# Attention heads one step deeper in the pipeline, and a bias by distance that goes through memory

## The chip, the cores and the metric

One core of a Trainium2 chip runs the whole program in one launch. The metric is device time in microseconds: 544.67 is the median of 3 runs of the kernel before (543.47 to 544.70). The engines are TensorE (PE; its weight loads are the row PEld), VectorE (DVE), ScalarE (ACT), GpSimd (POOL), and SyncE (SP), which issues the transfers.

## What is computed

Three stages, all in float32, with B=2, H=8, S=576, D=64, 32 hidden units:

```
scores = q @ k^T / sqrt(D)
x      = log1p(|i - j|) / log1p(max(i, 1))
bias   = relu(x * w1 + b1) @ w2            # for each head, row i and column j; the same for both batches
attn   = softmax(scores + bias);  o = attn @ v
y      = (o @ w_a * (o @ w_b)) @ w_out     # 1152 tokens, 512 -> 1536 -> 512
out    = LN(h * softmax(h)) * g @ w_out2,  h = y @ w_in    # 512 -> 1024 -> 512
```

Only the first stage is touched by the change. Its bias depends on the row i and the distance |i - j|.

## The kernel before

**Units and steps.** The 576 rows are four tiles of 128 and a tail of 64. A unit is one tile with one batch (the tail takes both batches), nine in all; a step is one head of one unit, 72 in all. A loop over n (line 635) walks the steps and in each emits parts in the order of a string (`ORDER`, line 27): a letter stands for one part, applied to the head of n or of some steps earlier. Each engine executes its instructions in the order in which they were emitted.

**One head.** `scores` (letter s, head n) makes the scores in PSUM (L400). `biased` (b, head n-1) adds the bias tile on VectorE and takes the minimum (the signs are turned), tile `e` (L419). `powers` (p, n-1) is the exponential with its row sum on ScalarE (L426). `summed_powers` (a, n-1) puts the sum into `rec` on GpSimd (L430). `shares` (h, n-2) takes the reciprocal on VectorE (L435) and multiplies the row by it on GpSimd (L436). `turned` (t, n-3) transposes on TensorE (L444, L453) and copies to SBUF. `values` (v, once in two steps) multiplies by V for two heads (L473). `scores` and the bias sums share a pool of two PSUM slots (`ps_s`).

**The bias.** It is made for 16 rows at a time; such a set is called T, 36 in all (8 to a tile, 4 in the tail). `bias_hidden` makes four hidden tiles of 128 x 576 from windows of a table `tabs` (L356 on VectorE, L358 on ScalarE, by the letters v and a of `HIDDEN`: 3 and 1 for T 0 to 7, all four on VectorE for T 8, 18 of 28 on VectorE for T 9 to 15, 28 of 32 for T 16 to 31, 14 of 16 for the rest). `bias_sums` sums them over the hidden units: 4 x 2 matmuls of 288 columns into one PSUM slot, four of them side by side in groups of 32 columns of the array (L366). `bias_out` scales them into SBUF (`st`, L376) and SP sends them to the bias tile, SBUF to SBUF, 288 KB (L385; twice for the tail). Two bias tiles exist (`big`). Tile 0 is made before the steps begin; T 9 to 15 have their sums at steps 5, 7, 9, 10, 12, 13, 14 (`SECOND_T`), T 16 on every second step from 16 to 46, the last four at 48, 50, 52, 54 (`LAST_T`). The hidden parts come one and two steps ahead of the sums, `bias_out` one step behind.

**Around it.** K, V and q are fetched by SP in the same queue. K is doubled on VectorE and transposed on TensorE until step 11. In the last unit the first expert weights are unpacked (`first_one`), and three products of the second stage (`gated`, L132) are emitted at steps 72, 74 and 75, among the last heads (`EARLY`).

Of the kernel before, what the change touches and what calls it, by code (L numbers as in the profile page):

```python
# [54 lines left out]
def tile_kernel(ctx, tc, q, k, v, w1, b1, w2, w_a, w_b, w_out, w_in2, w_out2, g_ln, psi, rpsi, out):  # L55
# [108 lines left out]
    with ExitStack() as actx:  # L164
# [35 lines left out]

        def table(a, n, row, at, pool, tag):

            w = (n + 1) // 2
            halves = []
            for i in range(2):
                m = min(w, n - i * w)
                ps = pool.tile([P, 512], F32, tag=tag, name=f"table_{a}_{i}")
                for g in range(4):
                    o = a + i * w - 4 * g - at
                    nc.tensor.matmul(ps[g * HID:(g + 1) * HID, 0:m], w1r, row[:, o:o + m], start=True, stop=True)  # L210
                halves.append((tb[:, a + i * w:a + i * w + m], ps[:, 0:m]))
            return halves

        halves_r = table(half, UW - half, psi_r, half - 12, ps_s, "s")
# [127 lines left out]
        def place(T):  # L342

            it, r = divmod(T, P // 16)
            return it, 64 * (r // 4), r % 4

        def bias_hidden(T, quads=range(4)):

            it, r, c = place(T)
            for qd in quads:  # L350
                t0 = it * P + r + 16 * qd
                h = hp.tile([P, S], F32, tag="h", name=f"h_{T}_{qd}")
                win = tb[:, OFF - t0 - c:OFF - t0 - c + S]
                sc = nb[:, c, t0 // 16:t0 // 16 + 1]
                if HIDDEN[min(it, 2)][T % len(HIDDEN[min(it, 2)])][qd] == "v":
                    nc.vector.tensor_scalar(h, win, sc, 0.0, op0=ALU.add, op1=ALU.max)  # L356
                else:
                    nc.scalar.activation(h, win, AF.Relu, bias=sc)  # L358
                bias_w.setdefault(T, []).append(h)

        def bias_sums(T):

            bps = ps_s.tile([P, 2, 512], F32, tag="s", name=f"bps_{T}")
# [5 lines left out]
        def bias_out(T, send=True):  # L369

            it, r, c = place(T)
            if it not in bias_t:
                bias_t[it] = big.tile([P, H, S], F32, tag="big", name=f"bias_{it}")
            st = stp.tile([P, S], F32, tag="st", name=f"st_{T}")
            k = 9 * c + 2 * it + r // 64
            nc.scalar.activation(st.rearrange("p (a j) -> p a j", a=2), bias_w.pop(T)[:, :, 0:SH], AF.Copy, scale=rp[:, k:k + 1])  # L376
            bias_w[T] = st
            if send:
                bias_sent(T)

        def bias_sent(T):
            it, r, c = place(T)
# [102 lines left out]

        units = [(it, [b]) for it in range(NC) for b in range(B)] + [(NC, list(range(B)))]

        qs = {}
        extra, sums_at, out_at, keep_at, low_at = {}, {}, {}, {}, {}

# [21 lines left out]
        for w in first_in:  # L512
            fetch(w)
        nc.sync.dma_start(psi_l, psi[3:4, low + 3 - 12:half + 3])
        N0 = P // 16
        for T in range(N0 + 2):
            if T == N0:
                nc.scalar.copy(*halves_l[0])
                nc.vector.tensor_copy(*halves_l[1])
            if T <= N0:  # L520
# [5 lines left out]
            if T == N0 - 2:  # L526
                halves_l = table(low, half - low, psi_l, low - 12, ps_t, "t")
            if T > 0:
# [471 lines left out]
```

## Time and profile before

| | us |
|---|---|
| median of 3 runs | 544.67 |
| the profiled execution | 544.01 |
| its span, first to last instruction | 542.2 |
| TensorE busy | 530.4 |
| VectorE busy | 419.1 |
| ScalarE busy | 286.1 |
| GpSimd busy | 156.5 |

The granted clock of TensorE is 1.0 of full speed all along. A matmul's end is modelled, so a TensorE that is busy all the time is not necessarily at its peak; the times from start to start say more. In the span the first bias and K are made until 27.8 us, the heads run until 212.4 us, and the other stages fill the rest.

### The profile page before, as it was taken

The page shows a single profiled execution, that of the slowest core. Times are in us where ns is not written, and L with a number is a line of the kernel's source. Part 1 is how long each engine was busy: PE and PEld are TensorE (multiplying, and loading weights), DVE is VectorE, ACT ScalarE, POOL GpSimd, SP SyncE. Part 2 cuts the span into 40 slices and gives each one's busy share as a digit, 9 for nine tenths or more (in the row PEclk, how much of TensorE's full clock was granted, in tenths as well). Part 3 has the DMA queues.
Part 4 walks back from the last instruction along what each step waited for, and adds up shares of the span by engine and source line. Part 5 has one row for each costly group of instructions (what it writes and reads, how often), then busy time and mean ns, then how long its engine had stood idle before and what let it go on. Part 6 is the DMA issues. An engine that isn't in the chain of part 4 may idle for free.

```text
span 542.2 us, 12391 instructions
## 1 busy us (share of the span) xinstructions
PE 530.4 (98%) x4873; PEld 471.8 (87%) x4873; DVE 419.1 (77%) x904; ACT 286.1 (53%) x598; POOL 156.5 (29%) x262
## 2 busy tenths in 40 slices
PE   7989999999999999999999999999999999999997
PEld 3667788888878899999999999999999988888886
DVE  5988889999886794887899798897884467656661
ACT  5878887788886663555565334522534332232321
POOL 3034445554456630222222122242224330000000
PEclk9999999999999999999999999999999999999999
DMA  4995533333266012444553443444300000000011
GB/s 93 208 197 127 115 82 86 78 73 79 69 151 181 3 41 82 154 144 128 156 153 121 117 155 117 128 144 152 118 4 2 0 1 20 21 19 21 19 31 48
DMA packets 53918, 49.32 MB, mean 91 GB/s; under 512 B 31583, under 2 KB 44132, under 8 KB 53861
## 3 DMA queue, kind: packets, MB, share of 16 engines
q1 hardware_dynamic: 53584, 48.52, 33.1%
q8 instruction: 38, 0.62, 0.5%
q14 instruction: 20, 0.16, 0.1%
q10 hardware_dynamic: 276, 0.02, 0.0%
HBM read 34.37 MB, written 2.36 MB: 68 GB/s over the span
## 4 chain that ended last, share of the span: by engine, by line
PE 83%; DVE 8%; issue 3%; ACT 3%; POOL 1%; DMA 1%; SPq 0%; ACTq 0%; DVEq 0%; POOLq 0%
PE pm L132 26%; PE po L132 11%; PE py L897 9%; PE ph L837 9%; PE bps L366 6%; PE px L473 6%; PE s L400 5%; PE pt L444 5%; DVE e L419 2%; PE pl L878 1%; ACT e L426 1%; PE tp_q L290 1%; DVE et L449 1%; PE tp_k L290 1%; DMA arena_hi<-in_k_dram 1%
## 5 line engine op out<-in xcount | busy, mean ns | idle before, releaser
L102 POOL TENSOR_SCALAR f<-f 128x512 f32<-128x512 f32 x48 | 41.5, 866 | 138.3 <-ACT f L98 127.3
L132 PE MATMUL pm<-xhi,abh 128*128 128x384 f32 x240 | 80.2, 334 | 0.0
L132 PE MATMUL pm<-xhi,abl 128*128 128x384 f32 x240 | 80.2, 334 | 0.0
L132 PE MATMUL pm<-xlo,abh 128*128 128x384 f32 x240 | 80.2, 334 | 0.0
L426 ACT ACTIVATE e<-e,nm 128x576 f32<-128x576 f32 x72 | 56.0, 777 | 32.2 <-DVE nm L419 30.8
L436 POOL TENSOR_SCALAR e<-e,rec 128x576 f32<-128x576 f32 x72 | 53.8, 747 | 28.7 <-DVE rec L435 26.2
L419 DVE CUSTOM_DVE_ANT_0 e<-s,bias 128x576 f32<-128x576 f32 x72 | 53.9, 750 | 2.6 <-DMA arena_hi<-in_k_dram 1.3
L356 DVE TENSOR_SCALAR h<-tabs 128x576 f32<-128x576 f32 x116 | 55.0, 515 | 0.3
L132 PE MATMUL po<-gh,oh 128*128 128x384 f32 x144 | 48.5, 337 | 0.8 <-DVE x2s L768 0.8
L151 ACT COPY one<-pm 128x384 f32<-128x384 f32 x36 | 17.2, 478 | 60.9 <-PE pm L132 60.7
L132 PE MATMUL po<-gh,ol 128*128 128x384 f32 x144 | 48.4, 336 | 0.0
L132 PE MATMUL po<-gl,oh 128*128 128x384 f32 x144 | 48.4, 336 | 0.0
L366 PE MATMUL bps<-h,w2bd 128*32 128x288 f32 x576 | 45.7, 420 | 1.2 <-DVE h L356 1.0
L444 PE MATMUL pt<-ident,e 128*128 128x128 f32 x288 | 45.1, 279 | 0.4 <-POOL e L436 0.4
L132 PEld LDWEIGHTS pm<-xhi,abl 128*128 128x128 f32 x240 | 45.1, 188 | 0.0
L132 PEld LDWEIGHTS pm<-xhi,abh 128*128 128x128 f32 x240 | 45.0, 188 | 0.0
L132 PEld LDWEIGHTS pm<-xlo,abh 128*128 128x128 f32 x240 | 45.0, 188 | 0.0
L114 DVE SCALAR_TENSOR_TENSOR f<-words,f 128x512 int32<-128x512 int32 x48 | 42.8, 891 | 1.6
L430 POOL TENSOR_SCALAR rec<-sums 128x1 f32<-128x1 f32 x72 | 20.9, 290 | 79.2 <-ACT e L426 78.9
L400 PE MATMUL s<-kst,qhi 128*128 128x288 f32 x160 | 40.6, 335 | 2.4 <-DVE nm L419 2.4
L473 PE MATMUL px<-et,vsb 128*32 128x128 f32 (+1 forms) x1280 | 40.5, 264 | 0.2 <-DVE et L449 0.2
L473 PEld LDWEIGHTS px<-et,vsb 128*32 128x32 f32 x1280 | 33.8, 110 | 7.5 <-issue 2.1
(137 smaller groups left out, 1247.8 us busy)
## 6 DMA issues: line engine op xcount, KB each, us to landing
bias<-st SPq DMA_DIRECT2D x40, 288.0 KB, 3.6
words<-in_moe_w_out_dram SPq DMA_DIRECT2D x20, 512.0 KB, 3.6
words<-in_moe_w_a_dram SPq DMA_DIRECT2D x12, 512.0 KB, 3.6
words<-in_moe_w_b_dram SPq DMA_DIRECT2D x12, 512.0 KB, 3.4
words<-in_moe_w_in_dram SPq DMA_DIRECT2D x8, 512.0 KB, 3.7
nat_q<-in_q_dram SPq DMA_DIRECT2D x16, 128.0 KB, 3.2
arena_hi<-in_k_dram SPq DMA_DIRECT2D x16, 128.0 KB, 2.5
vsb<-in_v_dram SPq DMA_DIRECT2D x16, 128.0 KB, 2.6
```

The source lines that it names most:

```text
L114: nc.vector.scalar_tensor_tensor(out=b, in0=words[:, :, 0], scalar=29, in1=b, op0=ALU.logical_shift_right, op1=ALU.bitwise_or)
L132: nc.tensor.matmul(ps, w, x, start=(i == 0), stop=(i == n - 1))
L356: nc.vector.tensor_scalar(h, win, sc, 0.0, op0=ALU.add, op1=ALU.max)
L366: nc.tensor.matmul(bps[32 * qd:32 * qd + 32, a, 0:SH], w2bd, h[:, a * SH:(a + 1) * SH], start=True, stop=True)
L400: nc.tensor.matmul(ps[:, a, 0:SH], w, kst[:, b, h, a * SH:(a + 1) * SH], start=(m == 0), stop=(m == len(mm) - 1))
L419: nc.vector.tensor_tensor_reduce(out=halves(e), in0=ps[:, :, 0:SH], in1=halves(bias_t[it][:, h, :]), op0=ALU.add, op1=ALU.min, scale=1.0, ...
L426: nc.scalar.activation(e, e, AF.Exp, bias=nm, scale=-1.0, accum_out=sums[:, h:h + 1])
L436: nc.gpsimd.tensor_scalar(e, e, rec[:, h:h + 1], 1.0, op0=ALU.mult, op1=ALU.mult)
L444: nc.tensor.transpose(pt[:, c, :], e[:, j * TL + c * P:j * TL + (c + 1) * P], ident)
L473: nc.tensor.matmul(px[rows, p, cols], lhsT, rhs, start=(c == 0 and m == 0), stop=(c == NC), skip_group_check=True)
L837: nc.tensor.matmul(ph[u][:, a], x[:, kc, cols], w[:, kc, a * 512:(a + 1) * 512], start=(i == 0), stop=(i == 3 * KD - 1))
L897: nc.tensor.matmul(ps, x[:, c, :], w[:, c, cols], start=(i == 0), stop=(i == 3 * KF - 1))
```

## The change

The heads get one more step: `shares` handles n-3, `summed_powers` n-2, `turned` n-4, `values` the pair of n-5, and the special orders of the first steps go. Tiles are taken in the order 0, 2, 1, 3, 4. For all T but those of tile 0, the hidden tiles hold one column for each distance from 0 on (d = max(before + 1, behind) columns, 319 to 576), made from one table that replaces the first one in `tabs`. The sums take one matmul of d columns (two where d is over 512). `bias_out` writes the distances forward and backward into a row of 636 columns, two instructions; SP sends these rows to a buffer in memory (318 KB), and two steps later reads 128 shifted rows of 576 from it into the bias tile (288 KB, twice for the tail). The steps of the sums move, and all four hidden tiles of T 8 to 31 are on VectorE.

```diff
-ORDER = {0: "kbvioljpatsxu", 2: "kbvioljptsxu", 3: "kbglfviojptshaxu", 4: "khbvioljpatsxu", 55: "khbilospajtvxu"}
+ORDER = {0: "hakbvimoljptsxu", 3: "kbhavimoljptsxu", 4: "hakbvimoljptsxu", 55: "hakbilmospjtvxu"}
-SECOND_T = (5, 7, 9, 10, 12, 13, 14)
-LAST_T = (48, 50, 52, 54)
+SECOND_T = (5, 6, 8, 9, 10, 11, 12)
+LAST_T = (45, 47, 49, 51)
+TILES = (0, 2, 1, 3, 4)
 HIDDEN = (("vvva", "vvva", "vvva", "vvva", "vvva", "vvva", "vvva", "vvva"),
-          ("vvvv", "avvv", "avav", "avvv", "avav", "avvv", "avav", "avvv"), ("vvvv", "avvv"))
+          ("vvvv",), ("vvvv",), ("vvvv",), ("vvvv", "avvv"))
...
+        dp = actx.enter_context(tc.tile_pool(name="dp", bufs=4, space=bass.MemoryType.DRAM))
...
+        def reach(T):
+            _, it, r, c = place(T)
+            t0 = it * P + r + c
+            return t0 + 60, S - t0
...
-                h = hp.tile([P, S], F32, tag="h", name=f"h_{T}_{qd}")
-                win = tb[:, OFF - t0 - c:OFF - t0 - c + S]
+                a, d = (OFF - half - t0 - c, S) if n == 0 else (0, max(before + 1, behind))
+                h = hp.tile([P, S], F32, tag="h", name=f"h_{T}_{qd}")[:, 0:d]
+                win = tb[:, a:a + d]
...
-                for a in range(2):
-                    nc.tensor.matmul(bps[32 * qd:32 * qd + 32, a, 0:SH], w2bd, h[:, a * SH:(a + 1) * SH], start=True, stop=True)
+                d = h.shape[1]
+                for a in range(0, d, 512):
+                    cols = slice(a, min(d, a + 512))
+                    nc.tensor.matmul(bps[32 * qd:32 * qd + 32, cols], w2bd, h[:, cols], start=True, stop=True)
...
-            nc.scalar.activation(st.rearrange("p (a j) -> p a j", a=2), bias_w.pop(T)[:, :, 0:SH], AF.Copy, scale=rp[:, k:k + 1])
...
+            nc.scalar.activation(st[:, before:W], bps[:, 0:behind], AF.Copy, scale=rp[:, k:k + 1])
+            nc.scalar.activation(st[:, 0:before], bps[:, before:0:-1], AF.Copy, scale=rp[:, k:k + 1])
...
         def bias_sent(T):
-            it, r, c = place(T)
-            st = bias_w.pop(T)
-            for base in ((r,) if it < NC else (0, TL)):
-                nc.sync.dma_start(bias_t[it][base + c:base + 64:4], st)
+            st, bias_w[T] = bias_w[T], dp.tile([P, W], F32, tag="bd", name=f"bd_{T}")
+            nc.sync.dma_start(bias_w[T], st)
+        def bias_in(T):
+            bd = bias_w.pop(T)[:, :]
+            for rows in bias_rows(T):
+                nc.sync.dma_start(rows, bass.AP(bd.tensor, bd.offset + 60, [[8 * W - 4, 16], [W, 8], [1, S]]))
...
-        nc.sync.dma_start(psi_l, psi[3:4, low + 3 - 12:half + 3])
...
-            later(7 + p, load_v, 1, p)
+            later(5 + p, load_v, 1, p)
...
-            n = LAST_T[r] if i == NC - 1 else 16 * i + (SECOND_T[r - 1] if i == 0 else 2 * r)
+            n = LAST_T[r] if i == NC - 1 else SECOND_T[r - 1] if i == 0 else 16 * i - 3 + 2 * r
...
             out_at.setdefault(n + 1, []).append(T)
+            in_at.setdefault(n + 3, []).append(T)
...
-        for n in range(len(steps) + 5):
+        for n in range(len(steps) + 6):
...
-                    if n >= 4 and n % 2 == 1:
-                        u, h = steps[n - 4]
+                    if n >= 6 and n % 2 == 0 and n - 5 < len(steps):
+                        u, h = steps[n - 5]
...
-                    f, j = {"b": (biased, 1), "h": (shares, 2), "g": (shares, 3), "f": (summed_powers, 2), "p": (powers, 1), "a": (summed_powers, 1), "t": (turned, 3), "s": (scores, 0)}[part]
+                    f, j = {"b": (biased, 1), "h": (shares, 3), "p": (powers, 1), "a": (summed_powers, 2), "t": (turned, 4), "s": (scores, 0)}[part]
```

## Rows read from the trace of the kernel before

**Rows 1.** Busy time by stage: microseconds and instructions of each engine, clock, DMA share, GB/s.
```profile
core 0: us, PE busy (x) PEld busy (x) DVE busy (x) ACT busy (x) POOL busy (x), PEclk, DMA share, GB/s
27.80:72.09 44.29, 42.24 (x576) 33.29 (x580) 37.74 (x103) 37.08 (x81) 16.68 (x35) 1.00 0.62 140
72.09:109.45 37.36, 37.36 (x612) 31.37 (x608) 34.53 (x91) 30.18 (x67) 18.91 (x37) 1.00 0.34 80
163.18:182.82 19.64, 19.37 (x292) 16.90 (x281) 12.75 (x38) 12.36 (x32) 12.48 (x27) 1.00 0.45 126
182.82:212.40 29.58, 29.10 (x545) 26.70 (x543) 23.30 (x55) 17.22 (x41) 9.99 (x20) 1.00 0.07 20
```

**Rows 2.** Timeline of TensorE, bias sums and products with V: start, length, instruction.
```profile
103.56 1.20 PE L366 MATMUL bps<-h,w2bd 128*32 128x288 f32 x16
104.56 1.08 PE L473 MATMUL px<-et,vsb 128*32 128x128 f32 x32
107.97 1.20 PE L366 MATMUL bps<-h,w2bd 128*32 128x288 f32 x16
...
112.83 1.20 PE L366 MATMUL bps<-h,w2bd 128*32 128x288 f32 x16
```

**Rows 3.** Timeline of one step without bias work; in brackets the idle time before.
```profile
170.04 0.74 DVE L419 CUSTOM_DVE_ANT_0 e<-s,bias 128x576 f32<-128x576 f32 x1
170.88 0.78 ACT L426 ACTIVATE e<-e,nm 128x576 f32<-128x576 f32 x1 [0.58 <-DVE nm L419]
171.83 0.19 POOL L430 TENSOR_SCALAR rec<-sums 128x1 f32<-128x1 f32 x1 [0.59 <-ACT e L426]
172.06 0.17 DVE L435 RECIPROCAL rec<-rec 128x1 f32<-128x1 f32 x1 [0.67 <-POOL rec L430]
172.18 0.76 DVE L419 CUSTOM_DVE_ANT_0 e<-s,bias 128x576 f32<-128x576 f32 x1
```

**Rows 4.** Timeline of VectorE: the biased scores of heads 12, 16, 56 and 64.
```profile
61.93 0.74 DVE L419 CUSTOM_DVE_ANT_0 e<-s,bias 128x576 f32<-128x576 f32 x1
...
72.09 0.76 DVE L419 CUSTOM_DVE_ANT_0 e<-s,bias 128x576 f32<-128x576 f32 x1 [0.25 <-PE bps L366]
...
165.85 0.74 DVE L419 CUSTOM_DVE_ANT_0 e<-s,bias 128x576 f32<-128x576 f32 x1
...
182.82 0.76 DVE L419 CUSTOM_DVE_ANT_0 e<-s,bias 128x576 f32<-128x576 f32 x1 [0.18 <-DVE rec L435]
```

**Rows 5.** Groups by line and shape: count, busy us, mean ns, idle before.
```profile
L356 DVE TENSOR_SCALAR h<-tabs 128x576 f32<-128x576 f32 x116 | 55.0, 515 | 0.3
...
L376 ACT ACTIVATE st<-bps,rp 128x576 f32<-128x576 f32 x36 | 26.7, 741 | 8.3 <-PE bps L366 8.0
...
L358 ACT ACTIVATE h<-tabs 128x576 f32<-128x576 f32 x28 | 21.8, 789 | 0.1
...
L455 ACT COPY ett<-ptt 128x128 f32<-128x128 f32 x36 | 9.0, 249 | 0.7 <-PE ptt L453 0.7
...
L119 DVE TENSOR_TENSOR ol<-f,oh 128x512 fp32r<-128x512 f32 x12 | 8.3, 688 | 0.0
...
L277 DVE TENSOR_SCALAR arena_lo<-arena_hi 128x256 fp32r<-128x256 f32 x8 | 2.3, 285 | 0.0
```

**Rows 6.** Busy time of a stretch of the early heads, columns as in Rows 1.
```profile
36.00:72.09 36.09, 35.30 (x502) 27.24 (x498) 31.06 (x85) 30.80 (x66) 13.53 (x28) 1.00 0.53 119
```

**Rows 7.** Transfers: destination and source, queue, count, KB each, median us to landing.
```profile
bias<-st SPq DMA_DIRECT2D x40, 288.0 KB, 3.6
...
out_dram<-osb SPq DMA_DIRECT2D x7, 256.0 KB, 2.0
```

**Rows 8.** The bias tile's transfers: issue time min/median/max in ns, landing.
```profile
L385 SPq DMA_DIRECT2D bias<-st x40: 532/532/953, 11.0 to 162.6; - x40
...
DMA to landing us min/median/max: 3.2/3.6/4.6
```

**Rows 9.** Timeline: the transposes of the last head, TensorE.
```profile
206.15 0.66 PE L444 MATMUL pt<-ident,e 128*128 128x128 f32 x4 [0.27 <-POOL e L436]
```

More of the change, by code (lines that the diff above doesn't have):

```diff
@@ L199, in tile_kernel, with table @@
         nc.scalar.activation(warm, ident[:, 0:1], AF.Exp)
-        def table(a, n, row, at, pool, tag):
+        def table(n, at, step, pool, tag):
             w = (n + 1) // 2
@@ L206, in table @@
                 m = min(w, n - i * w)
-                ps = pool.tile([P, 512], F32, tag=tag, name=f"table_{a}_{i}")
+                ps = pool.tile([P, 512], F32, tag=tag, name=f"table_{step}_{i}")
                 for g in range(4):
-                    o = a + i * w - 4 * g - at
-                    nc.tensor.matmul(ps[g * HID:(g + 1) * HID, 0:m], w1r, row[:, o:o + m], start=True, stop=True)
-                halves.append((tb[:, a + i * w:a + i * w + m], ps[:, 0:m]))
+                    o = at + i * w - step * g
+                    nc.tensor.matmul(ps[g * HID:(g + 1) * HID, 0:m], w1r, psi_d[:, o:o + m], start=True, stop=True)
+                halves.append((tb[:, i * w:i * w + m], ps[:, 0:m]))
             return halves
-        halves_r = table(half, UW - half, psi_r, half - 12, ps_s, "s")
+        halves = table(NX, 12, 4, ps_s, "s")
         ps_nb = ps_t.tile([P, 4, NG // 4], F32, tag="t", name="ps_nb")
@@ L342, in place @@
         def place(T):
[L344 to L345 removed]
+            n, r = divmod(T, P // 16)
+            return n, TILES[n], 64 * (r // 4), r % 4
+        def reach(T):
+            _, it, r, c = place(T)
+            t0 = it * P + r + c
+            return t0 + 60, S - t0
         def bias_hidden(T, quads=range(4)):
[L349 removed]
+            n, it, r, c = place(T)
+            before, behind = reach(T)
             for qd in quads:
                 t0 = it * P + r + 16 * qd
[L352 to L353 removed]
+                a, d = (OFF - half - t0 - c, S) if n == 0 else (0, max(before + 1, behind))
+                h = hp.tile([P, S], F32, tag="h", name=f"h_{T}_{qd}")[:, 0:d]
+                win = tb[:, a:a + d]
                 sc = nb[:, c, t0 // 16:t0 // 16 + 1]
[L355 removed]
+                if HIDDEN[n][T % len(HIDDEN[n])][qd] == "v":
                     nc.vector.tensor_scalar(h, win, sc, 0.0, op0=ALU.add, op1=ALU.max)
@@ L361, in bias_sums, with bias_rows, bias_out @@
         def bias_sums(T):
-            bps = ps_s.tile([P, 2, 512], F32, tag="s", name=f"bps_{T}")
+            bps = ps_s.tile([P, 2, 512], F32, tag="s", name=f"bps_{T}").rearrange("p a j -> p (a j)")
             for qd, h in enumerate(bias_w[T]):
-                for a in range(2):
-                    nc.tensor.matmul(bps[32 * qd:32 * qd + 32, a, 0:SH], w2bd, h[:, a * SH:(a + 1) * SH], start=True, stop=True)
+                d = h.shape[1]
+                for a in range(0, d, 512):
+                    cols = slice(a, min(d, a + 512))
+                    nc.tensor.matmul(bps[32 * qd:32 * qd + 32, cols], w2bd, h[:, cols], start=True, stop=True)
             bias_w[T] = bps
-        def bias_out(T, send=True):
-            it, r, c = place(T)
+        def bias_rows(T):
+            _, it, r, c = place(T)
             if it not in bias_t:
                 bias_t[it] = big.tile([P, H, S], F32, tag="big", name=f"bias_{it}")
-            st = stp.tile([P, S], F32, tag="st", name=f"st_{T}")
-            k = 9 * c + 2 * it + r // 64
-            nc.scalar.activation(st.rearrange("p (a j) -> p a j", a=2), bias_w.pop(T)[:, :, 0:SH], AF.Copy, scale=rp[:, k:k + 1])
+            return [bias_t[it][base + c:base + 64:4] for base in ((r,) if it < NC else (0, TL))]
+        def bias_out(T, send=True):
+            n, it, r, c = place(T)
+            before, behind = reach(T)
+            st = stp.tile([P, W], F32, tag="st", name=f"st_{T}")
+            bps = bias_w.pop(T)
+            k = 9 * c + 2 * it + r // 64
+            if n == 0:
+                nc.scalar.activation(st[:, 0:S], bps[:, 0:S], AF.Copy, scale=rp[:, k:k + 1])
+                for rows in bias_rows(T):
+                    nc.sync.dma_start(rows, st[:, 0:S])
+                return
+            nc.scalar.activation(st[:, before:W], bps[:, 0:behind], AF.Copy, scale=rp[:, k:k + 1])
+            nc.scalar.activation(st[:, 0:before], bps[:, before:0:-1], AF.Copy, scale=rp[:, k:k + 1])
             bias_w[T] = st
@@ L381, in bias_sent @@
         def bias_sent(T):
-            it, r, c = place(T)
-            st = bias_w.pop(T)
-            for base in ((r,) if it < NC else (0, TL)):
-                nc.sync.dma_start(bias_t[it][base + c:base + 64:4], st)
+            st, bias_w[T] = bias_w[T], dp.tile([P, W], F32, tag="bd", name=f"bd_{T}")
+            nc.sync.dma_start(bias_w[T], st)
+        def bias_in(T):
+            bd = bias_w.pop(T)[:, :]
+            for rows in bias_rows(T):
+                nc.sync.dma_start(rows, bass.AP(bd.tensor, bd.offset + 60, [[8 * W - 4, 16], [W, 8], [1, S]]))
         st_ = {}
@@ L484, in inputs_low @@
             nc.vector.tensor_tensor(out=xlo, in0=px, in1=xhi.bitcast(F32), op=ALU.subtract)
-        units = [(it, [b]) for it in range(NC) for b in range(B)] + [(NC, list(range(B)))]
+        units = [(it, [b]) for it in TILES[:NC] for b in range(B)] + [(TILES[NC], list(range(B)))]
         qs = {}
-        extra, sums_at, out_at, keep_at, low_at = {}, {}, {}, {}, {}
+        extra, sums_at, out_at, in_at, keep_at, low_at = {}, {}, {}, {}, {}, {}
         def later(n, f, *args):
@@ L526, in tile_kernel @@
             if T == N0 - 2:
-                halves_l = table(low, half - low, psi_l, low - 12, ps_t, "t")
+                halves = table(S, 12 + OFF - half, 0, ps_t, "t")
             if T > 0:
@@ L633, in at @@
                 f(*steps[n])
-        for n in range(len(steps) + 5):
+        for n in range(len(steps) + 6):
             for part in ORDER[max(i for i in ORDER if i <= n)]:
-                if part == "o":
+                if part == "m":
+                    for T in in_at.get(n, []):
+                        bias_in(T)
+                elif part == "o":
                     for T in out_at.get(n, []):
@@ L640, in tile_kernel @@
                 elif part in "ij":
-                    if n >= 12 and n % 8 == 4:
+                    if n >= 13 and n % 8 == 5:
                         (inputs_high if part == "i" else inputs_low)(n // 8 - 1)
```

27 lines of the change are left out of this document (14 added, 13 removed).

## The prediction

> **What bounds the kernel now.** First the busy time by stage [rows 1]: from 72.09 to 109.45 us TensorE is busy all of 37.36 us, VectorE 34.53, ScalarE 30.18, GpSimd 18.91. A busy TensorE may only be waiting, so next its timeline: a pair of heads with one set of bias sums takes 112.83 - 107.97 = 4.86 us where q is transposed and 107.97 - 103.56 = 4.41 us where not, and the sums hold the engine 104.56 - 103.56 = 1.00 us until the next work starts [rows 2]. Without bias work a pair should then take 3.41 us, 3.86 with q. It does not: the eight heads from 165.85 to 182.82 us take 16.97 us [rows 4], 4.24 per pair. The chain of one such step shows why [rows 3]: biased scores at 170.04, exponential 170.88, sum picked up by GpSimd 171.83, reciprocal 172.06, and only behind that reciprocal, on the same VectorE queue, the next biased scores at 172.18. That ring takes 2.14 us per head whatever TensorE could do. So there are two bounds: TensorE's work where bias sums run, the ring where none do. From 27.8 to 72.09 us the two mix with transfers: TensorE has 2.05 us without work, and the DMA engines are 62% busy [rows 1].
>
> **Part 1, shorter sums (lines 361 to 367).** A set now has d columns per quad. The d of T 9 to 15 add up to 319+319+320+381+382+383+384 = 2488, or 4.32 x 576: of 7 sets 2.68 are saved. T 16 to 23: 381 to 384 and 445 to 448, 3316 in all = 5.76 x 576, 2.24 of 8 saved. T 24 to 31: 445 to 448 and 509 to 512, 3828 = 6.65 x 576, 1.35 of 8. The tail: 573 to 576, nothing. At 1.00 us a set [rows 2] that is 6.3 us. Bounds: nothing, if a set costs the same whatever its length, and 23 x 0.5 = 11.5 us, if it costs by its matmuls, of which half go. I take 6.3, because the four side-by-side groups stream columns. T 8 is made before the heads, where tile 0's transfer ends last; nothing is counted for it.
>
> **Part 2, one step more between sum and reciprocal.** The reciprocal ahead of the biased scores of one head now belongs to a head two earlier, whose sum GpSimd has put down a step before. The ring [rows 3] then spans two steps, some 1.07 us per head, below everything else. Heads 56 to 63 fall to TensorE's work: two pairs at 3.41 and two at 3.86 are 14.5 us instead of 16.97 [rows 2, 4], 2.4 less; GpSimd (12.48 busy of 19.64 us [rows 1]) comes closer to full, so I take 2.0 of it. Bounds 0 and 2.4. In the stage with sums the ring had slack against 4.41, so no gain there.
>
> **Part 3, VectorE and ScalarE.** All hidden tiles of T 9 to 31 go to VectorE. Before, 74 of 92 were there, 74 x 0.515 = 38.1 us. A one-source instruction takes 0.285 us at 256 columns and 0.515 at 576 [rows 5], so 0.356, 0.399 and 0.445 at the mean lengths 355, 414 and 478: 28 x 0.356 + 32 x 0.399 + 32 x 0.445 = 37.0 us. VectorE keeps its load, in pairs that are 0.17 to 0.38 us shorter; it was busy 92% of them [rows 1] and comes to 96%, in an order that leaves little play. I put 0.5 us for that (0 to 4, see the rivals). ScalarE loses 18 x 0.789 = 14.2 us. It gains an instruction for each of 27 sets: from 0.249 us at 128 and 0.741 at 576 columns [rows 5], 1.10 ns a column and 0.11 us fixed, two of 636 columns together take 0.92, 0.18 more than now, 4.8 us in all. The second reads PSUM backward, which no row shows; from no change to four times its columns (some 0.9 us a set more) it stays under ScalarE's 19% of idle time plus what it loses. Nothing for it.
>
> **Part 4, the bias through memory.** SP issues 28 transfers more, 0.53 us each [rows 8], 15 us of queue time in 150. Behind a read that waits for its write stand the writes of the next set and q's and V's fetches; a write has two steps, some 4.7 us, and lands in about 3.6 (3.2 to 4.6) [rows 7, 8], so the queue mostly doesn't stop. The one tight date is T 15: sums at step 12, rows scaled at 13, read asked for at 15, head 16 biased at 17. That leaves four steps, now 72.09 - 61.93 = 10.2 us [rows 4], perhaps 9.6 after. It needs 0.3 + 0.9 of ScalarE and twice 3.6 to 4.6: 8.4 to 10.4 us. Later tiles have three steps more. Also the DMA engines get fuller: 0.53 x 36.09 = 19.1 us of work between 36 and 72 us [rows 6]. A bias transfer costs at most 0.34 x 37.36 / 8 = 1.6 us of them (eight sets and four q fetches there) [rows 1], so eight more and T 16's make up to 14, 33 us in a stretch of some 33: full, without play. I take 1.0 us of lateness at head 16; bounds 0 and, if a transfer costs much more through memory, 14 (below).
>
> The row for a transfer from SBUF into memory is the output's: 256 KB land in 2.0 us on quiet queues [rows 7], against 3.6 for 288 KB inside SBUF. The Trainium skill (DMA: Bandwidth & Descriptors, section "Anatomy of one DMA — SWDGE (gpsimd) path") gives about 2.0 us plus bytes at 436 GB/s, and warns that a write's receipt can be surprisingly long when the target is memory; an estimate from it is 2.75 us for a write of 318 KB. By that T 15 would be in time and the sum 1.0 us lower; the rows of busy queues speak for the later date.
>
> **Part 5, the two ends.** At the start the pipeline fills one step longer: one head's transposes and half a pair's products, about 1.1 us of TensorE's work (half of 3.41 less the scores), wait a step longer, partly while the engine has nothing else: 0.5 us lost (0 to 1.1). Against it, heads 4 to 12 lose ScalarE's 10 hidden tiles (7.9 us in a stage where it is 84% busy) and the ring; of TensorE's 2.05 us without work [rows 1] I take 1.5 back. With part 4's 1.0 the early stage comes out even. At the end the last heads stand between `gated` products, which TensorE does in any case; only 0.27 us is lost there before [rows 9], and one more step of lag is filled by the same products: nothing. The last unit (29.10 busy of 29.58 us [rows 1]) has the ring too, but VectorE has the expert weights in it: 0.5 us gained (0 to 1.2).
>
> **Sum.** -6.3 - 2.0 + 0.5 (VectorE) + 1.0 + 0.5 - 1.5 (early stage) - 0.5 (last unit) = -8.3 us. Made against the profiled execution, 544.01 us (span 542.2 and 1.8 around it), that is 535.7; the median of the runs is 0.66 higher, so 536.4 us. The stages behind the heads don't change and only move.
>
> **Rivals.**
>
> A. *Memory is late: slower.* Place: steps 4 to 17. The DMA work there is 19.1 us less its eight copies (12.8), 6.3, plus 17 transfers at x us each. At x = 1.6 it fits (33 us). If writing to and reading from memory costs x = 2.4, it is 47 us, head 16 waits 14 us: 536.4 + 14 = 550. It turns slower than 544.7 where the wait passes 8.3 us, at x = 2.06. For it: the DMA share from 27.8 to 72 us is 0.62 already, 0.34 after it [rows 1], and no transfer of this kernel has gone through memory. Against: x = 1.6 is an upper price already, as the q fetches are in it, and 256 KB into memory land in 2.0 us [rows 7]. In a milder form (x about 1.8) 3 to 4 us are lost: 540.
>
> B. *VectorE becomes the bound.* Half the sets have an odd d. If an odd length loses the fast form that a one-source instruction has (0.515 us at 576 against 0.688 at 512 for a two-source one [rows 5]), each such tile costs 1.47 times as much: 0.47 x 37.0 / 2 + 1.9 in the tail = 10.6 us more of VectorE, of which half shows, as it has only a few per cent of play: 541. Against: nothing in the rows, no odd one-source tile is there. The Trainium skill (VectorE: DVE Perf Modes, section "What auto-detection actually checks") allows the two-port form where the outermost counts are even or equal, and they are equal here; by that B falls away. No row here shows it.
>
> C. *The ring stays* (something else holds the reciprocal back, such as the products on GpSimd ahead of the sums in its queue): part 2 and the gains at both ends fail, 540.
>
> D. *More goes than counted.* If all idle time of the early stage goes (2.05), memory is in time, the last unit gains 1.2, VectorE costs nothing and part 2 gives its 2.4: 536.4 - 0.5 - 1.0 - 0.5 - 0.7 - 0.4 = 533.3.
>
> **Chances.** Forecast 0.45; D 0.19; B 0.13; C 0.07; A mild 0.08, A slower than before 0.08. About 0.3% (1.6 us) is what a measurement here can tell from no change: faster than 543.0 in all of the forecast, C, D, nearly all of B and most of mild A, 0.87; within, 0.05; slower than 546.3, 0.08. The range reaches from under D to the upper end of B: 532.5 to 541.5.
>
> **What would show it.** Starts of the sums and of the next products 0.55 to 0.89 us apart in place of 1.00 by length: part 1. Heads 56 to 63 at 1.8 us each, and no wait of the reciprocal for GpSimd: part 2. Head 16's biased scores waiting for a transfer: A; if not, the 1.0 us was too much. Hidden tiles on VectorE near 0.36 to 0.45 us, odd and even alike: part 3; odd ones near 0.6: B. Wrong altogether if pairs with short sums still take 4.4 us or more with TensorE waiting for VectorE.

## Result and profile after

The changed kernel takes 548.24 us (median of 6 runs, 546.05 to 548.57) against 544.10 (542.92 to 545.05) before: ratio 1.0071, 95% interval 1.0049 to 1.0092. The forecast was 536.4. The profiled execution took 548.35 us, its span is 546.2 instead of 542.2.

The table cuts the span at the starts of biased scores; "71-end" reaches from those of head 71 to the fourth `gated` block, the first behind the three early ones, from which on all kernels issue the same work (325 to 327 us). Each row is one profiled execution, in us; the last column is the median of the runs:

| | to 0 | 0-12 | 12-16 | 16-48 | 48-56 | 56-64 | 64-71 | 71-end | span | median |
|---|---|---|---|---|---|---|---|---|---|---|
| before | 27.8 | 34.1 | 10.2 | 75.0 | 18.8 | 17.0 | 17.4 | 16.4 | 542.2 | 544.1 |
| after | 28.3 | 36.1 | 9.9 | 74.2 | 17.4 | 15.9 | 19.5 | 19.0 | 546.2 | 548.2 |
| e1 pipeline only | 27.7 | 33.8 | 11.2 | 74.4 | 17.4 | 15.9 | 19.5 | 19.0 | 545.8 | 547.6 |
| e2 bias only | 28.0 | 34.7 | 9.2 | 75.0 | 18.3 | 17.0 | 17.5 | 16.4 | 541.2 | 543.6 |
| e3 old drain | 27.6 | 34.3 | 10.0 | 74.2 | 17.4 | 15.9 | 19.5 | 17.9 | 542.1 | 545.8 |
| e4 ScalarE's share | 28.3 | 33.8 | 10.0 | 74.2 | 17.4 | 15.9 | 19.5 | 19.0 | 543.9 | 546.7 |
| e5 q one earlier | 28.6 | 38.5 | 9.6 | 76.2 | 16.3 | 20.9 | 19.7 | 19.0 | 554.8 | 555.1 |
| e6 low half behind copy | 27.9 | 34.5 | 9.9 | 74.5 | 17.6 | 17.5 | 20.7 | 19.0 | 547.7 | 551.7 |
| e7 back before last unit | 27.7 | 34.7 | 10.0 | 74.2 | 17.4 | 17.8 | 17.7 | 16.4 | 541.2 | 544.0 |
| e8 e4 + e6 + e7 | 27.9 | 33.6 | 9.8 | 76.5 | 17.6 | 19.1 | 17.7 | 16.4 | 544.0 | 545.5 |
| e9 e6 + write first | 27.5 | 35.3 | 11.1 | 72.5 | 17.4 | 16.0 | 19.5 | 19.0 | 544.5 | 546.3 |
| e10 e9 + e7 | 27.8 | 34.7 | 10.7 | 72.5 | 17.4 | 17.8 | 17.7 | 16.4 | 540.3 | 542.9 |
| e11 e10 + e4 | 28.8 | 33.6 | 10.8 | 72.5 | 17.4 | 17.8 | 17.7 | 16.4 | 540.3 | 542.1 |
| e12 write first only | 28.7 | 36.0 | 10.7 | 74.0 | 17.4 | 16.0 | 19.4 | 19.0 | 547.3 | 548.9 |

Read across the first two rows, the change gains 0.8 us in heads 16 to 48 and 2.4 in heads 48 to 64, and loses 2.0 in each of heads 0 to 12 and 64 to 71 and 2.6 behind head 71. The 0.5 ahead of head 0 is scatter: e3 to e12 issue the same instructions up to there as the changed kernel and reach head 0 at 27.5 to 28.8 us.

Busy time by stage after, columns and first stretches as in [rows 1]:

```profile
core 0: us, PE busy (x) PEld busy (x) DVE busy (x) ACT busy (x) POOL busy (x), PEclk, DMA share, GB/s
28.29:74.31 46.02, 41.25 (x501) 30.87 (x502) 39.75 (x118) 33.76 (x80) 14.88 (x32) 0.96 0.83 199
74.31:111.16 36.85, 36.64 (x538) 29.12 (x537) 33.18 (x95) 29.45 (x71) 16.80 (x37) 1.00 0.52 151
...
58.00:60.00 2.00, 1.36 (x12) 0.94 (x16) 1.84 (x4) 1.69 (x5) 0.42 (x2) 0.91 0.93 280
60.00:62.00 2.00, 2.00 (x32) 1.23 (x28) 0.86 (x4) 0.93 (x3) 0.00 (x0) 0.50 0.65 186
62.00:64.00 2.00, 2.00 (x31) 1.61 (x24) 1.54 (x6) 1.19 (x4) 1.24 (x3) 0.74 0.45 164
```

The early heads now use 0.83 of the DMA engines (0.62 before), and TensorE stands still for 4.77 us (2.05 before). From 59.6 to 63.0 us its granted clock is 0.50, the lower of its two levels, 1.2 instead of 2.4 GHz.

The timeline of a pair after, all engines; it answers to [rows 2]:

```profile
88.97 0.69 DVE L330 SCALAR_TENSOR_TENSOR qlo<-tp_q,qhi 128x512 fp32r<-128x512 f32 x1 [0.30 <-ACT qhi L317]
89.32 0.85 PE L379 MATMUL bps<-h,w2bd 128*32 128x383 f32 x8
89.58 0.68 DVE L479 COPY et<-pt 128x512 f32<-128x512 f32 x1
89.98 1.29 PE L503 MATMUL px<-et,vsb 128*32 128x128 f32 x30
90.31 0.69 PEld L503 LDWEIGHTS px<-et,vsb 128*32 128x32 f32 x26 [0.21 <-DVE et L479]
...
91.53 0.65 PE L474 MATMUL pt<-ident,e 128*128 128x128 f32 x4
...
93.72 0.85 PE L379 MATMUL bps<-h,w2bd 128*32 128x382 f32 x8
94.38 1.06 PE L503 MATMUL px<-et,vsb 128*32 128x128 f32 x32
```

The sums hold TensorE 89.98 - 89.32 = 0.66 us, as a length of 383 of 576 would have it. But the pair still takes 93.72 - 89.32 = 4.40. The products behind the sums start, and their weight loads (PEld) then wait for the copy of the second head's transposed powers (`et`, L479), which VectorE does behind the low half of q (`qlo`, L330, what the rounded `qhi` leaves of q): from the products' start to the next transposes it is 91.53 - 89.98 = 1.55 us, 1.22 before. So it is in every pair in which q is not transposed (no turn of q): the products grow to 1.34, 1.45, 1.56 us where the sums shrink to 0.88, 0.77, 0.66.

VectorE's biased scores of heads 12, 16, 56 and 64, as in [rows 4]:

```profile
64.36 0.76 DVE L449 CUSTOM_DVE_ANT_0 e<-s,bias 128x576 f32<-128x576 f32 x1 [0.82 <-PE s L430]
...
74.31 0.76 DVE L449 CUSTOM_DVE_ANT_0 e<-s,bias 128x576 f32<-128x576 f32 x1 [0.17 <-PE s L430]
...
165.87 0.76 DVE L449 CUSTOM_DVE_ANT_0 e<-s,bias 128x576 f32<-128x576 f32 x1
...
181.80 0.76 DVE L449 CUSTOM_DVE_ANT_0 e<-s,bias 128x576 f32<-128x576 f32 x1 [0.25 <-DVE rec L465]
```

Heads 12 and 16 wait for their scores, not for a transfer.

Groups by line and shape, as in [rows 5], and the transfers of lines 409 and 415, as in [rows 8]:

```profile
L367 DVE TENSOR_SCALAR h<-tabs 128x446 f32<-128x446 f32 x8 | 3.4, 462 | 0.0
...
L367 DVE TENSOR_SCALAR h<-tabs 128x447 f32<-128x447 f32 x8 | 3.3, 457 | 0.0
...
L401 ACT ACTIVATE st<-bps,rp 128x446 f32<-128x446 f32 x1 | 0.6, 633 | 0.1
...
L402 ACT ACTIVATE st<-bps,rp 128x446 f32<-128x446 f32 x1 | 0.6, 626 | 0.0
```

```profile
L415 SPq DMA_DIRECT2D bias<-bd x32: 532/538/600, 39.9 to 167.5; - x32
L409 SPq DMA_DIRECT2D bd<-st x28: 320/542/2128, 36.1 to 162.4; - x28
...
DMA to landing us min/median/max: 2.7/3.8/5.3
```

At these lengths an odd one (447) costs VectorE what an even one does (446), and one ScalarE instruction that reads PSUM backward (L402) takes 626 ns, forward 633.

### The profile page after: what moved, and what is told of

It reads as the page before. It is cut to its first block, busy times and chain, and to the rows that moved or that the text cites. A ratio compares the mean times of both kernels' runs of the same rounds, so it can differ in the third digit from the quotient of the medians.

```text
span 546.2 us, 12091 instructions
## 1 busy us (share of the span) xinstructions
PE 530.0 (97%) x4681; PEld 465.0 (85%) x4681; DVE 416.5 (76%) x922; ACT 281.4 (52%) x608; POOL 151.1 (28%) x262
## 4 chain that ended last, share of the span: by engine, by line
PE 83%; DVE 7%; ACT 4%; issue 3%; DMA 2%; SPq 0%; POOL 0%; DVEq 0%; ACTq 0%
PE pm L134 25%; PE po L134 11%; PE py L931 9%; PE ph L871 9%; PE px L503 7%; PE s L430 6%; PE bps L379 5%; PE pt L474 5%; PE tp_q L293 2%; PE pl L912 1%; PE tp_k L293 1%; DVE et L479 1%; DVE e L449 1%; DMA words<-in_moe_w_out_dram 1%; ACT e L456 1%
## 5 line engine op out<-in xcount | busy, mean ns | idle before, releaser
L449 DVE CUSTOM_DVE_ANT_0 e<-s,bias 128x576 f32<-128x576 f32 x72 | 53.7, 746 | 9.9 <-PE s L430 7.9
L367 DVE TENSOR_SCALAR h<-tabs 128x576 f32<-128x576 f32 (+17 forms) x134 | 55.8, 463 | 2.8 <-PE bps L379 2.2
L503 PEld LDWEIGHTS px<-et,vsb 128*32 128x32 f32 x1280 | 34.9, 111 | 14.8 <-issue 9.1
L474 PE MATMUL pt<-ident,e 128*128 128x128 f32 x288 | 44.8, 278 | 1.5 <-POOL e L466 1.5
L503 PE MATMUL px<-et,vsb 128*32 128x128 f32 (+1 forms) x1280 | 44.0, 268 | 0.8 <-DVE xlo L514 0.4
L100 ACT ACTIVATE f<-words 128x512 f32<-128x512 f32 x48 | 32.5, 676 | 17.2 <-DMA words<-in_moe_w_out_dram 7.3
L379 PE MATMUL bps<-h,w2bd 128*32 128x512 f32 (+17 forms) x384 | 40.1, 491 | 1.2 <-DVE h L367 1.2
```

The source lines that it names most:

```text
L379: nc.tensor.matmul(bps[32 * qd:32 * qd + 32, cols], w2bd, h[:, cols], start=True, stop=True)
L449: nc.vector.tensor_tensor_reduce(out=halves(e), in0=ps[:, :, 0:SH], in1=halves(bias_t[it][:, h, :]), op0=ALU.add, op1=ALU.min, scale=1.0, ...
L474: nc.tensor.transpose(pt[:, c, :], e[:, j * TL + c * P:j * TL + (c + 1) * P], ident)
L503: nc.tensor.matmul(px[rows, p, cols], lhsT, rhs, start=(c == 0 and m == 0), stop=(c == NC), skip_group_check=True)
```

## Experiments

Two theories after the result. S: the order of the work; the added step leaves more work behind the last head and brings instructions together on VectorE that other engines wait for. M: the way through memory; transfers late, queue full.

**The two parts alone (e1, e2).** e1 has the new lags with the bias of before, its sums a step earlier; e2 the new bias with the lags and the order of before.

```diff
# e1, on before
-            n = ... 16 * i + (SECOND_T[r - 1] if i == 0 else 2 * r)
+            n = ... (SECOND_T[r - 1] if i == 0 else 16 * i - 1 + 2 * r)
+ORDER, "h" 3, "a" 2, "t" 4, values of n - 5, inputs at n % 8 == 5: as after
# e2, on after
-LAST_T = (45, 47, 49, 51)
+LAST_T = (46, 48, 50, 52)
-            n = ... 16 * i - 3 + 2 * r
+            n = ... 16 * i - 2 + 2 * r
+ORDER with "m" ahead of "o", lags: as before
```

> The added step alone, with the bias of before (sums moved by one step so that they stand in the pair as before). Theory S (the loss lies in the order of work: the step that is added leaves more of TensorE's work behind the last head, and puts the copies of q and of the transposed scores into the same step on VectorE): slower than before, by 2 to 4 us, about 547; after head 71 some 2.6 us more than before, heads 56 to 63 about 1 us less. Theory M (the bias through memory is what costs, the added step gains): faster than before by about 2 us, 542.

> The bias by distance and through memory alone, with the pipeline of before. Theory S: heads 16 to 48 faster by 2 to 3 us from the shorter sums, the stretch from the last head to the end as before, heads 6 to 16 still slower than before by up to 2 us as the sums stand in five steps one after the other: 541 to 544. Theory M: slower than before, 547 to 549, most of it in heads 6 to 16.

e1: 547.63 us, ratio 1.0070 (1.0046 to 1.0095). e2: 543.63, 0.9991 (0.9980 to 1.0002). So the step alone makes a loss as large, and the bias gains next to nothing on its own: M falls. The two losses are alike from head 64 on (4.6 us in e1, 4.7 in the changed kernel), not in the rest: e1 loses 1.0 us in heads 12 to 16 and 1.4 behind the last column's cut, the changed kernel 2.0 in heads 0 to 12. For e2, S had expected 2 to 3 us less in heads 16 to 48; they take the same 75.0. The sums shrink there as well, but the timeline of TensorE puts another wait in the place of what they save:

```profile
84.42 0.85 PE L379 MATMUL bps<-h,w2bd 128*32 128x384 f32 x8
...
88.79 0.85 PE L379 MATMUL bps<-h,w2bd 128*32 128x383 f32 x8 [0.25 <-DVE nm L449]
```

The sums wait for biased scores (L449): sums and scores share two PSUM buffers, and the old lags keep the ring of [rows 3]. That this takes the whole saving is argued; no run takes it apart.

**Drain and share (e3, e4).** e3 drains the last heads from step 72 on with the old lags; e4 gives ScalarE its old hidden tiles.

```diff
# e3: the loop over steps ends at N + 5, with parts "x" alone from N = 72
+drain = {N: (shares N-3, summed_powers N-2, biased and powers N-1, turned N-4, values of pair 1, shares N-2, summed_powers N-1),
+         N + 1: (shares N-1, turned N-3 and N-2, values of pair 2), N + 2: turned N-1, N + 3: values of pair 3, N + 4: inputs}
# e4
-          ("vvvv",), ("vvvv",), ("vvvv",), ("vvvv", "avvv"))
+          ("vvvv", "avvv", "avav", "avvv", "avav", "avvv", "avav", "avvv"), ("vvvv", "avvv"), ("vvvv", "avvv"), ("vvvv", "avvv"))
```

> The changed kernel, with the last heads drained at the lags of before from step 72 on (nothing else differs). Theory S: the stretch from head 71 to the second stage falls by 2.0 to 2.6 us, 545.8. If that stretch is long for another reason (the order of the expert weights on VectorE earlier in the last unit), less than 1 us.

> The changed kernel, with ScalarE making its old share of the hidden tiles (10 of T 9 to 15, 4 of each later eight). Theory S with VectorE's pile-up in heads 6 to 12: these heads become 1.5 to 2.5 us shorter, TensorE's clock stays at full, 546. Theory M (full DMA queues hold the early heads): no difference there, 548.

e3: 545.77, 1.0035 (1.0015 to 1.0055); e4: 546.73, 1.0051 (1.0033 to 1.0069). The old drain takes back 1.2 of the 2.6 us behind head 71, where 2.0 to 2.6 were expected; that the time still came out at the 545.8 expected is luck, in part from the clock (below). With 2.4 us less work on VectorE between 74 and 148 us, e4's heads 16 to 48 take the same 74.2: VectorE's amount of work doesn't hold them. Its gain lies ahead of head 12 (33.8 us instead of 36.1), but not as expected: heads 0 to 6 take 13.3 us instead of 14.2, while heads 6 to 12, which were to gain, take 20.50, no less than in e3 (20.31); the rest is the clock.

e3 also prices the clock. Up to step 72 it is the changed kernel, with the same wait (1.02 us, at 57.8), but in its profiled execution the clock stayed up:

```profile
60.00:62.00 2.00, 2.00 (x40) 1.53 (x32) 2.00 (x9) 1.48 (x5) 0.95 (x2) 1.00 0.56 186
```

Heads 6 to 12 take 20.31 us there and 21.87 in the changed kernel's: 1.6 us of the 2.0 lost in heads 0 to 12 are clock. By the executions' mean clocks most of this is in the median too. All six executions of the changed kernel have a mean granted clock of 0.997, as its profiled one; of ten of e3, six have 0.996 or 0.997 (median 546.4) and four 1.000 (545.1), and e7 further down divides in the same way, 545.0 and 543.3. Where the clock fell is known of the profiled executions alone, and it matters: e7's fell from 30.2 to 33.6 us, and its heads 0 to 12 take 34.7 us, e3's 34.3. With ScalarE's old share (e4, e8, e11) 20 of 21 executions have 0.999 or more: that the tiles moved to VectorE bring the fall is likely, but not shown.

**VectorE's order (e5, e6).** Theory V: what holds heads 16 to 48 is the copy behind the low half of q. Theory R: the two PSUM buffers, or VectorE's load.

```diff
# e5
-                later(8 * u - 3 + 4 * g, twice, w)
-                load_at(8 * u - 2 + 4 * g, w)
+                later(8 * u - 4 + 4 * g, twice, w)
+                load_at(8 * u - 3 + 4 * g, w)
# e6
-... 4: "hakbvimoljptsxu", 55: "hakbilmospjtvxu"}
+... 4: "hakbvimojptlsxu", 55: "hakbimospjtlvxu"}
```

> The changed kernel, with the doubling and the turn of each q block of units 1 to 8 one step earlier, so that its low half (DVE qlo, 0.69) falls into the steps in which VectorE has no copy of transposed powers. In the changed kernel a pair of heads without a turn keeps 4.40 us whatever its sums cost, because the products grow by what the sums shrink (1.23 us to 1.34, 1.45, 1.56 while the sums went 0.99, 0.88, 0.77, 0.66). Theory V (VectorE's order: the copy of the pair's second head stands behind the low half of q): these pairs fall to 4.07 to 4.29, heads 16 to 48 from 74.2 to about 72 us in sum, heads 64 to 71 by 0 to 1, the time from 548.2 to about 546. Theory R (a ring of the two buffers that scores and sums share, or VectorE's whole load): the pairs stay at 4.40 and the wait moves to the sums (PE bps from DVE nm), 548.

> The changed kernel, with one letter of its order moved: the low half of q (l) is issued behind the transposes and their copy (t) of the same step, from step 4 on; nothing else. Theory V: as in the run with q one step earlier, pairs without a turn 4.07 to 4.29 us instead of 4.40, heads 16 to 48 about 72 us in sum instead of 74.2, time 546; pairs with a turn stay at 4.5 to 4.7. Theory R: 4.40 stays, 548. If the low half comes too late for its scores, PE waits for it at the first head of every half unit (s from DVE qlo), up to 0.7 each.

e5: 555.12, 1.0199 (1.0147 to 1.0252); e6: 551.70, 1.0158 (1.0111 to 1.0205). V is borne out in the pairs and both times are wrong: pairs without a turn take 4.05 to 4.31 us in both where the sums are shorter, products 1.21, but now the bias comes late. e6, VectorE and SP's queue ahead of head 48 (146.77):

```profile
133.18 0.54 SPq L415 DMA_DIRECT2D bias<-bd  x1
133.77 0.58 SPq L409 DMA_DIRECT2D bd<-st  x1
137.84 0.54 SPq L415 DMA_DIRECT2D bias<-bd  x1
138.47 1.36 SPq L409 DMA_DIRECT2D bd<-st  x1
...
142.46 0.54 SPq L415 DMA_DIRECT2D bias<-bd  x1
...
146.77 0.76 DVE L449 CUSTOM_DVE_ANT_0 e<-s,bias 128x576 f32<-128x576 f32 x1 [1.99 <-DMA bias<-bd]
```

Each read stands on SP until its own write, issued 4 us ahead, has landed, and the next write stands behind the read: 4.6 us a set, more than a pair now takes (4.55 on average from 73.2 to 141.4 us). In e5 head 32 waits 3.55 us for its bias, and two turns of q wait 6.1 us in all for GpSimd's doubling, around each of which the granted clock was 0.50 for 6.8 us. e6 pays besides 3.5 us where scores wait for the low half, most of it from head 54 on, where no bias work is. Its four executions took 549.7 to 555.2 us, the two longer ones with a mean clock of 0.994; the trace is of one of the shorter.

**Back before the last unit (e7), and e4, e6 and e7 together (e8).** From step 63 on, e7 has the lags and order of before.

```diff
+            if n == 63:
+                at(shares, n - 3)
+                at(summed_powers, n - 2)
+                at(turned, n - 4)
-            for part in ORDER[max(i for i in ORDER if i <= n)]:
+            for part in ORDER[max(i for i in ORDER if i <= n)] if n < 63 else "khbilospajtvxu":
+... lags of "h", "a", "t" and of values one less, inputs at n % 8 == 4, from 63 on
```

> The changed kernel, but from step 63 on (heads 62 and later, and the whole last unit and drain) with the lags and the order of the kernel before; up to there nothing differs. Theory S (the added step itself costs in the last unit and behind the last head): heads 64 to 71 from 19.46 to 17.4 to 18 us, last head to the fourth early gated block from 19.03 to 16.4 to 17, so the time from 548.2 to 544 (543.5 to 545). If it is the earlier bias or products that hold the last unit: heads 64 to 71 stay at 19.4.

> The changed kernel with three edits at once: low half of q behind the copy, lags of before from step 63 on, and ScalarE's old share of the hidden tiles (546.73 alone). If the costs are separate they add: 548.2 - 1.5 - 2 - 4 = 540.7 us (539.5 to 542.5), below the kernel before; heads 16 to 48 about 72 us, heads 64 to 71 about 17.5, last head to the fourth early gated block about 16.5. If ScalarE then binds where VectorE did, heads 16 to 48 stay at 74.2 and the time is about 542.7.

e7: 543.98, 1.0005 (0.9987 to 1.0022). As expected, heads 64 to 71 are back at 17.7, the end at 16.4. Not expected: the step back costs 1.8 at head 64, where the work behind one head is caught up. The stretches from head 56 on so gain 2.5 us in all; that the time fell by 4.3, to the 544 expected, is in part luck, as the early heads, which have the same instructions, took 34.7 us instead of 36.1. e8: 545.49, 1.0017 (1.0008 to 1.0027), where 540.7 was expected: two heads wait 2.7 and 1.5 us for transfers of the bias, as in e6.

**The queue (e9 to e12).** One letter more: the next write is issued ahead of the read. e9 is e6 with that (the low half stays put from step 55), e10 adds e7, e11 also e4; e12 is the changed kernel with that alone.

```diff
-... 4: "hakbvimoljptsxu", 55: "hakbilmospjtvxu"}
+... 4: "hakbviomjptlsxu", 55: "hakbilmospjtvxu"}   # e9, e10, e11
+... 4: "hakbviomljptsxu", 55: "hakbilmospjtvxu"}   # e12
```

> The run with the low half of q behind the copy took the wait of the products away (pairs without a turn 4.05 to 4.31 us), but head 48 then stood 1.99 us for its bias: SP's queue is in order, each read of memory waits there for its own write to land (about 4.0 us), and the next set's write stands behind it, so one set took 4.62 to 4.8 us while a pair of heads takes 4.1 to 4.6. Here the same kernel (from step 4; from step 55 the low half stays where the changed kernel has it) issues the next write ahead of the read. Theory Q (the queue's order): no bias is waited for any more, heads 16 to 48 72 us or less in sum (74.2 in the changed kernel), heads 56 to 64 15.9, time 546 (545 to 547). Theory L (the transfers themselves land late because the heads are faster): head 48 still waits 1 us or more, heads 16 to 48 73.5 to 74.5, time 548.

> As the run before in this list, and with the lags and the order of the kernel before from step 63 on (543.98 when done alone). Theory Q: the two add, 543.98 - 2.2 = 541.8 us (541 to 543), a span of 539, faster than the kernel before. Theory L: 543.5 to 544.5, no gain over the kernel before.

> As the run before in this list, and with ScalarE's old share of the hidden tiles (546.73 against 548.24 for the changed kernel, all of it ahead of head 16). If VectorE's pile-up ahead of head 16 is what that share relieves: 0.8 to 1.5 below the run before in this list, 540.5 us. If ScalarE's copies then come late to the sums and scores in heads 16 to 48 (37.26 and 39.21 us in the run with three edits): the same as the run before or up to 1 slower.

> The changed kernel with nothing but the next write ahead of the read (from step 4). No head of the changed kernel waits for its bias for more than 0.4 us and its reads are issued every 4.26 to 4.28 us, in time with the pairs, so by every theory nothing moves: heads 16 to 48 74.2 us in sum with pairs without a turn at 4.40, the time 547 to 548.5. If it is below 547 the queue cost something in the changed kernel too.

e9: 546.32, 1.0044 (1.0027 to 1.0060). e10: 542.92, 0.9980 (0.9968 to 0.9991). e11: 542.13, 0.9967 (0.9954 to 0.9980). e12: 548.89, 1.0088 (1.0070 to 1.0105). Theory Q holds: heads 16 to 48 take 72.5 us and none behind head 16 waits for its bias; e12 gains nothing (547 to 548.5 expected), so the queue costs something only once the products no longer wait. The gains don't simply add: e10 is 1.1 us below e7, where 2.2 were expected, and e11 0.8 below e10. In all four, heads 12 to 16 take 0.7 to 1.2 us more than in the changed kernel; in e10 and e11 head 16 waits 1.0 and 1.1 us for its bias, whose read is issued 0.7 and 0.9 us later behind head 12 than there, and for e9 and e12 this stays open. e11 beats both kernels, by 1.9 us (544.01 for the kernel before beside it) and 6.1. Its sums and products on TensorE, two pairs:

```profile
87.92 0.85 PE L379 MATMUL bps<-h,w2bd 128*32 128x383 f32 x8
88.59 1.06 PE L503 MATMUL px<-et,vsb 128*32 128x128 f32 x32
...
91.98 0.85 PE L379 MATMUL bps<-h,w2bd 128*32 128x382 f32 x8
...
96.49 0.85 PE L379 MATMUL bps<-h,w2bd 128*32 128x381 f32 x8
```

4.06 us without a turn of q and 4.51 with one, 0.35 less each than in [rows 2]; these are pairs with the shortest sums.

## Why the prediction was wrong

Against the forecast, heads 0 to 16 were to gain 2.7 us and lost 1.7, heads 16 to 48 to gain 3.1 and gained 0.8, heads 48 to 64 to gain 2.0 and gained 2.4, the last unit to gain 0.5 and lost 2.0, the end was to cost nothing and cost 2.6. Parts 1 and 5 failed; the largest misses are the last unit with the end (5.1 us) and the early heads (4.4).

**Part 1, the step that failed first.** It took the sums as lying wholly on TensorE's path, 6.3 us, because they hold TensorE 1.00 us from start to start in a stage in which it has no idle time [rows 1, 2]. The lengths were right (0.66, 0.77, 0.88 us for 1.00 x d/576). Heads 16 to 48, of which 3.6 was expected, gave 0.8. Pairs with a turn of q got the whole saving (4.51 to 4.72 instead of 4.85), pairs without one nothing, pairs with `inputs_low` (VectorE takes the low part of a finished unit's products from PSUM) less than nothing (5.04 to 5.22; 4.90 to 5.05 before). The reason is shown by e5, e6, e9: VectorE's order had the copy ready for the products only as long as the sums were long. The prediction named the sign ("pairs with short sums still take 4.4 us or more with TensorE waiting for VectorE") but gave the order 0.5 us, from busy shares, without walking one pair. Even with the order mended e9 gains 2.5 of the 3.6: its pairs with `inputs_low` still take 5.1 to 5.2 us, 1.53 to 1.81 of it products. That the weight loads there wait for the copy and for the low part of the products is in the trace; it wasn't taken apart further.

**Part 2 had the mechanism right and twice its size.** In the changed kernel's timeline the reciprocal is no longer behind this head's own exponential:

```profile
172.12 0.15 DVE L465 RECIPROCAL rec<-rec 128x1 f32<-128x1 f32 x1
172.19 0.74 DVE L449 CUSTOM_DVE_ANT_0 e<-s,bias 128x576 f32<-128x576 f32 x1
...
173.42 0.16 DVE L465 RECIPROCAL rec<-rec 128x1 f32<-128x1 f32 x1 [0.48 <-POOL rec L460]
173.54 0.76 DVE L449 CUSTOM_DVE_ANT_0 e<-s,bias 128x576 f32<-128x576 f32 x1
```

Two heads start 1.35 us apart, and heads 56 to 64 take 15.93 us instead of 16.97: 1.0 us went where 2.0 were forecast. Every second reciprocal now waits 0.48 us for GpSimd, and the 14.5 of TensorE's work alone isn't reached; what holds these heads now wasn't taken apart. That 2.4 us went from head 48 on is luck: 1.4 of it lies in heads 48 to 56 (e1 has it too), for which the prediction gave nothing.

**Part 3.** Hidden tiles of 446 and 447 columns take 0.46 us, odd as even, where the interpolation gives 0.42 (for T 9 to 31 in all 40.8 us instead of 37.0): rival B falls. The second instruction of `bias_out`, priced at nothing, isn't free in the early heads (part 5).

**Part 4.** Rival A falls: in the changed kernel only head 0 waits for a transfer (0.4 us), and head 16 isn't late, so the 1.0 us put there was too much. Transfers land in 3.8 us (2.7 to 5.3). The estimate of 2.75 us for a write, worked out from the Trainium skill (DMA: Bandwidth & Descriptors, section "Anatomy of one DMA — SWDGE (gpsimd) path"), is not met by these on their busy queue. But the step that "the queue mostly doesn't stop" held only at the changed kernel's slow pace; in e6 the queue was the next bound.

**Part 5 failed at both ends.** "The early stage comes out even" on top of shorter sums; it lost 1.7 us between heads 0 and 16. 1.6 of that is the clock: e3 and e7, with the same instructions there, take 44.4 and 44.8 us, before 44.3. The other miss is the 2.7 us of shorter sums. TensorE did save them, but as waits: in e3 it stands still for 4.81 of the 44.39 us, 2.05 before. Two of its waits in the changed kernel, both in these heads alone (us in total, times, longest):

```profile
PE s L430 <- ACT st L402: 1.5, 3, 0.7
PE tp_k L293 <- DVE qlo L330: 1.0, 1, 1.0
```

Three times the scores wait for `bias_out`'s second instruction (L402), which still reads a PSUM slot that they share with the sums. And to read three steps behind, sums run on steps 8 to 12 one after the other, and VectorE has in one step hidden tiles, a low half and a copy that TensorE waits for:

```profile
57.90 0.68 DVE L330 SCALAR_TENSOR_TENSOR qlo<-tp_q,qhi 128x512 fp32r<-128x512 f32 x1
58.51 0.67 DVE L479 COPY et<-pt 128x512 f32<-128x512 f32 x1
58.63 1.05 PE L293 MATMUL tp_k<-ident,nat_k 128*128 128x128 f32 x8 [1.03 <-DVE qlo L330]
```

Then the clock fell. The last unit, "0.5 us gained", lost 2.0, the end, "nothing", lost 2.6, in e1 as well. The timeline of VectorE after, in the last unit and behind it:

```profile
187.87 0.76 DVE L330 SCALAR_TENSOR_TENSOR qlo<-tp_q,qhi 128x256 fp32r<-128x256 f32 x2 [1.03 <-ACT qhi L317]
188.67 0.69 DVE L479 COPY et<-pt 128x512 f32<-128x512 f32 x1
189.28 0.68 DVE L115 SCALAR_TENSOR_TENSOR single<-words,single 128x512 int32<-128x512 int32 x1
190.00 0.69 DVE L116 SCALAR_TENSOR_TENSOR single<-words,single 128x512 int32<-128x512 int32 x1
190.61 0.15 DVE L465 RECIPROCAL rec<-rec 128x1 f32<-128x1 f32 x1
...
205.02 0.69 DVE L116 SCALAR_TENSOR_TENSOR single<-words,single 128x512 int32<-128x512 int32 x1
205.63 0.16 DVE L465 RECIPROCAL rec<-rec 128x1 f32<-128x1 f32 x1
...
213.58 0.69 DVE L479 COPY et<-pt 128x512 f32<-128x512 f32 x1 [4.98 <-PE pt L474]
214.19 1.28 DVE L642 TENSOR_TENSOR first<-single,first 128x512 fp32r<-128x512 f32 x2
```

In the last unit the added step puts the low half and the copy into the same step, ahead of the expert weights and of the reciprocal. Behind the last head the reciprocals stand behind the weights, and the last copy, a step later now, waits 4.98 us behind `gated` products with the next block's weights (L642) in the queue behind it. TensorE pays for both; it answers to [rows 9]:

```profile
206.76 0.66 PE L474 MATMUL pt<-ident,e 128*128 128x128 f32 x4 [0.70 <-POOL e L466]
...
214.93 0.61 PE L134 MATMUL pm<-xhi,first 128*128 128x384 f32 x2 [0.92 <-DVE first L642]
```

These two waits are 1.6 us, where 0.27 was before [rows 9]; the other 1.3 us behind head 71 weren't taken apart. The filler was there as the prediction said; what it left out is that a lag also moves each instruction past others in VectorE's queue. e7 shows that the added step makes these losses; that they come from VectorE's order is read from the timeline, not shown by a run.

## What to carry over

A TensorE that shows no idle time in a stage may still owe its length to another engine's order: before pricing shorter matmuls, walk one pair of the timeline and ask which operand arrives last for the work behind them. A pipeline step more moves every stage past others in the in-order queues and is paid again at each end, so list what each moved instruction now stands ahead of and behind, and go back to the old lags where there is nothing to gain. When a bound goes, compute the next: here an in-order DMA queue in which a read waits for its write took 4.6 us per set in e6, which did no harm under pairs of 74.2 / 16 = 4.64 us on average and bound once they could take 72.5 / 16 = 4.53. And check a time that comes out as forecast stretch by stretch: e3 and e7 met theirs with other stretches than expected.

## What the hardware showed

After TensorE had waited 1.03 us at 58.6, following shorter waits, its granted clock was 0.50 between 60 and 62 us and 0.74 over the next two; in e3, after the same instructions and a wait of 1.02 us, it stayed at 1.00. In e7 it was 0.50 from 30.2 to 33.6 us instead. An ACT read of PSUM in reverse order took 626 ns at 446 columns, forward 633.
